# Moving a block's first transform steps within a fused Fourier-mixing and SoLU kernel, and reordering the float64 conversion in its opening

## The chip, the cores and the metric

The kernel runs on one core of a Trainium2 chip. The metric is the device time of one execution in microseconds; a lower number is better. Seven runs of the kernel before took 1685.17 to 1698.09 us, with a median of 1690.2 us.

## What is computed

The reference has two parts. The first filters each of 8 sequences of 3136 tokens by 256 channels in the frequency domain. The second is a feed-forward layer on all 25088 tokens: a product with `w_in` (256 by 1024), softmax-weighting of each value by itself (SoLU), a layer norm with gain `g_ln`, and a product with `w_out` (1024 by 256).

```python
X = np.fft.rfft(x, axis=1)                  # x: 8 x 3136 x 256
y = np.fft.irfft(X * (filt_r + 1j * filt_i)[None], n=3136, axis=1)
h = y.reshape(25088, 256) @ w_in            # w_in, w_out arrive as float64
e = np.exp(h - h.max(-1, keepdims=True))
solu = h * e / (e.sum(-1, keepdims=True) + 1e-9)
ln = (solu - mean) / np.sqrt(var + 1e-6) * g_ln
out = ln @ w_out
```

## The kernel before

**Two kinds of work.** Each of the 8 sequences (an "entry", `e` = 0 to 7) goes through a Fourier transform that is written as small matrix products. A *first step* (a DFT of 49 points) works on one of 8 pieces of the sequence; its result is stored to a DRAM scratch tensor `d1`. Seven *spectrum units* read `d1`, transform (`forward`), multiply by the filter (`multiply`), transform back (`inverse`) and store to `d2`. Eight *steps back* (`fetch_back`, `back`) read `d2` and fill the token buffer `y`. The feed-forward layer then works on the tokens of `y`, 128 at a time.

**The opening** (L360 to L562) does the whole transform of entry 0, for there is nothing to overlap it with. Beside it, the two weight matrices, which lie in DRAM as float64, are converted to float32 in eight pieces `j` = 0 to 7, four for `w_in` and four for `w_out`. `begin(j)` issues the load of the raw 32-bit words from GpSimd's DMA queue into one of 3 buffers (`raw`). `load_float64` then builds the float32 from the words: eight VectorE instructions (L381 to L393) for sign, exponent and the upper bits of the fraction, and, in `finish`, one ScalarE instruction (L396) and two GpSimd instructions (L397, L398) for the lower bits. The conversions of pieces 2 to 7 stand between the steps back of entry 0, whose 16 products (`py`, L353) are each evacuated by ScalarE (L356). Ahead of the steps back stand seven "idle products" (`idle_row(7, "idler")`, L534), which compute nothing that is used.

**The steps.** After the opening, a loop of 205 steps (L988) runs the feed-forward layer, one block of 128 tokens per step, software-pipelined: in step `k`, TensorE makes the products with `w_in` for block `k` (L682; every two blocks share seven products of half blocks, for which GpSimd makes sums first, `pair_sums`, L660), ScalarE and VectorE apply the exponential and the normalisation to block `k-2`, VectorE transposes block `k-3` (L740), and DMAs regroup it (L752). The products with `w_out` (L794) begin only at step 9 (`LAG`). The order of everything within a step is written out by hand in `step(k)`, so each engine's instructions stand in that order.

**Where the transform of entries 1 to 7 stands.** `PLAN` gives, for each entry, the steps at which its eight first steps, seven spectrum units and eight steps back are put. Entry 2 (the third entry) has its first steps at steps 1, 3, ... 15. For entries 2 to 7 a first step at step `t` is made of these parts:

- four loads of rows of `x` from SyncE's DMA queue (`fetch_quarters`, L236), into one of four buffers (`r`) that steps back also use. The load is put about three steps ahead; a load due before step 0 is issued ahead of the loop;
- a subtraction on VectorE (`difference`, L245), at the beginning of step `t`, into the only buffer of its kind (`diff`);
- an addition on GpSimd (`sum`, L251), in the middle of step `t`;
- eight products on TensorE (`first_quarters`, L260), four with `x` and four with `diff`, and two copies on ScalarE (L265), at the end of step `t`;
- two stores to `d1` from GpSimd's DMA queue (L271), at the beginning of step `t+1`.

Entry 1 is different: its first steps (L217) stand in steps 0 and 1, its rows were loaded by SyncE in the opening (`fetch_second`, L415; the last two pieces by GpSimd, L206), and its results are stored by GpSimd's queue (L223). Between `fetch_second` and the first rows of entry 2, SyncE's queue stores the filter to DRAM (`f_dram`, L543).

**The output weights** are also prepared in the first four steps: in step 0 they are scaled by `g_ln` (L618), in step 1 their mean over rows is made by 32 products (`ps_mean`, L626), in step 2 it is subtracted (L631), in step 3 the sums of quarters are made (L141).

Of the kernel before, what the change touches and what calls it, by code (L numbers as in the profile page):

```python
# [9 lines left out]
FP32 = mybir.dt.float32  # L10
I32 = mybir.dt.int32
AFT = mybir.ActivationFunctionType
ALU = mybir.AluOpType
# [23 lines left out]
PLAN = [  # L37
    None,
    ([0, 0, 0, 0, 1, 1, 1, 1], [4, 5, 6, 7, 8, 10, 12], [16, 17, 18, 19, 20, 20, 21, 22]),
    (range(1, 17, 2), range(18, 32, 2), [34, 36, 38, 40, 42, 43, 44, 46]),  # L40
    ([17, 23, 25, 27, 29, 31, 33, 35], range(38, 52, 2), range(54, 70, 2)),
    (range(39, 55, 2), range(58, 72, 2), range(76, 92, 2)),
    (range(63, 79, 2), range(82, 96, 2), range(100, 116, 2)),
    (range(87, 103, 2), range(106, 120, 2), range(126, 142, 2)),
# [48 lines left out]
def kernel(  # L93
# [10 lines left out]
    nc = tc.nc  # L104
# [6 lines left out]
    def pool(name, bufs, space=None, stack=ctx):  # L111
        kw = {} if space is None else {"space": space}
        return stack.enter_context(tc.tile_pool(name=name, bufs=bufs, **kw))
# [15 lines left out]
    w_in_sb = consts.tile([P, 7, DFF // 2], FP32, name="w_in_sb")  # L129
# [8 lines left out]
    def weight_sums(w):  # L138

        for to, a, b in ((3, 6, 0), (5, 2, 6), (4, 2, 3), (6, 1, 4)):  # L140
            nc.vector.tensor_tensor(out=w[:, to], in0=w[:, a], in1=w[:, b], op=ALU.subtract)  # L141
# [218 lines left out]
    with ExitStack() as st:  # L360
        fpool = pool("fp", 1, stack=st)
        pools = {name: pool(name + "0", bufs, stack=st)
                 for name, bufs in (("r", 1), ("t2", 1), ("p", 2), ("g", 2))}
        wpool = pool("wp", 3, stack=st)
        ps_h = pool("ps_h", 3, PSUM, stack=st)

        def load_words(src, n):
# [3 lines left out]
                in_=src)  # L371
            return raw

        def load_float64(dst, raw, negate=False):


            lo, hi = raw[:, :, 0], raw[:, :, 1]
            power = wpool.tile([P, 512], I32, name="power", tag="power", bufs=2)
            frac = dst.bitcast(I32)
            ts, stt = nc.vector.tensor_scalar, nc.vector.scalar_tensor_tensor  # L380
            ts(out=lo, in0=lo, scalar1=8, scalar2=None, op0=ALU.logical_shift_right)  # L381
            rest = lo.bitcast(FP32)
            ts(out=power, in0=hi, scalar1=20, scalar2=0x7FF, op0=ALU.logical_shift_right,
               op1=ALU.bitwise_and)
            ts(out=power, in0=power, scalar1=896.0, scalar2=0.0, op0=ALU.subtract, op1=ALU.max)
            ts(out=power, in0=power, scalar1=255.0, scalar2=None, op0=ALU.min)
            ts(out=power, in0=power, scalar1=23, scalar2=-2 ** 31 if negate else 0,
               op0=ALU.logical_shift_left, op1=ALU.bitwise_or)
            stt(out=power, in0=hi, scalar=-2 ** 31, in1=power, op0=ALU.bitwise_and,
                op1=ALU.bitwise_xor)  # L390
            ts(out=frac, in0=hi, scalar1=0xFFFFF, scalar2=3, op0=ALU.bitwise_and,
               op1=ALU.logical_shift_left)
            nc.vector.tensor_tensor(out=frac, in0=frac, in1=power, op=ALU.bitwise_or)  # L393

            def finish():
                nc.scalar.mul(rest, lo, 2.0 ** -44)  # L396
                nc.gpsimd.tensor_tensor(out=rest, in0=rest, in1=power.bitcast(FP32), op=ALU.mult)  # L397
                nc.gpsimd.tensor_tensor(out=dst, in0=dst, in1=rest, op=ALU.add)  # L398

            return finish  # L400

        filters, tables = {}, {}

# [23 lines left out]
        weights = []  # L427
# [18 lines left out]
        raws = {}  # L446

        def begin(j):
            raws[j] = load_words(weights[j][1], j)
# [40 lines left out]
        def idle_row(count, name):  # L490
            for j in range(count):
                idle(ps_h.tile([P, 2, C], FP32, name=f"{name}_{j}", tag="h"))
# [1 line left out]
        idle_row(8, "idle")  # L494

        def convert(j):
            return load_float64(weights[j][0], raws.pop(j), negate=j < 4)

        for j in range(2):
            convert(j)()  # L500

        def start(i):
            sp.fetch_filter(i)
# [15 lines left out]
        for i in range(units):  # L519
            if i + 2 < units:  # L520
                start(i + 2)
            sp.multiply(i, 0, nc.vector.tensor_tensor)
            sp.multiply(i, 1, nc.gpsimd.tensor_tensor)
            pss = [ps_t.tile([P, 2, C], FP32, name=f"pc_0_{i}_{u}", tag="t") for u in range(2)]
            idle(pss[0])
            sp.inverse(i, pss)
            sp.store(i, nc.scalar.dma_start)
            if i == 0:
                nc.gpsimd.dma_start(out=wi_t, in_=wi_dram)
                nc.gpsimd.dma_start(out=wq_t, in_=wq_dram)  # L530
                nc.gpsimd.dma_start(out=g_sb, in_=moe_g_ln.rearrange("(k p) -> p k", p=P))
            elif i in (1, 3, 4):
                begin({1: 2, 3: 3, 4: 4}[i])
        idle_row(7, "idler")  # L534
        rows_t4 = pools["r"].tile([P, NH, C], FP32, name="t4_0", tag="r")
        for ch in range(pieces):
            t4s[0, ch] = rows_t4[0:NK, NCH * ch:NCH * ch + NCH]
# [3 lines left out]
        for i0, n, rows in ((0, 4, P), (4, 4, P), (8, NP - 9, P), (NP - 1, 1, NQ)):  # L541
# [1 line left out]
            nc.sync.dma_start(  # L543
                out=f_dram[i0:i0 + n].rearrange("i u q k c -> (u q) i (k c)")[0:rows],
                in_=f[0:rows, at:at + n].rearrange("p i k c -> p i (k c)"))

        rest = {2: convert(2)}
        rest.pop(2)()
        begin(5)
        rest[3] = convert(3)  # L550
        for ch in range(pieces):
            if ch in (0, 2, 4, 6):
                j = 3 + ch // 2
                rest.pop(j)()
                if j < 5:
                    begin(j + 3)
                rest[j + 1] = convert(j + 1)
                if j == 3:
                    weight_sums(w_in_sb)
            for cb in range(KD):  # L560
                back(0, ch, cb, nc.scalar.copy)
        rest.pop(7)()  # L562


    ps_b = [pool(f"ps_b{u}", 1, PSUM) for u in range(2)]
# [270 lines left out]
    for e in range(1, B):  # L836
# [5 lines left out]
        for i, t in enumerate(first_at):  # L842
            dma = nc.gpsimd.dma_start
            if e == 1:
                if i not in sp.xs:
                    row_loads.append((t, t - 1, -1, lambda sp=sp, i=i, dma=dma: sp.fetch_x(i, [dma] * 2)))
                for u in range(2):
                    (early, late)[u][t].append(lambda sp=sp, i=i, u=u: sp.first(
                        i, (u,), psum(f"pa_{sp.e}_{i}_{u}").rearrange("p a c -> p (a c)").rearrange(
                            "p (o n) -> p o n", o=1), nc.scalar.copy, sp.xs[i][0:NK, 2 * u:2 * u + 2, :]))  # L850
                    (early, late)[u][t].append(lambda sp=sp, i=i, u=u: sp.store_first(
                        i, 2 * u, nc.gpsimd.dma_start))
            else:

                assert t % 2
                row_loads.append((t, t - 2, -1, lambda sp=sp, i=i: sp.fetch_quarters(i, nc.sync.dma_start)))
                stores[t].append(lambda sp=sp, i=i: sp.difference(i))
                products[t].append(lambda sp=sp, i=i: sp.sum(i))
                late[t].append(lambda sp=sp, i=i: sp.first_quarters(
                    i, [psum(f"pa_{sp.e}_{i}_{g}") for g in range(2)]))  # L860
                stores[t + 1].append(lambda sp=sp, i=i, dma=dma: sp.store_quarters(i, dma))
# [158 lines left out]
```

## Time and profile before

| | us |
|---|---|
| median of seven runs | 1690.2 |
| lowest and highest of them | 1685.17, 1698.09 |
| the profiled execution, its device time | 1696.86 |
| its span in the profile | 1695.1 |
| TensorE busy | 1603.3 (95%) |
| VectorE busy | 1264.7 (75%) |
| GpSimd busy | 1125.6 (66%) |
| ScalarE busy | 939.6 (55%) |
| mean granted TensorE clock | 0.982 |

In stages of the same execution, again in microseconds:

| stretch | TensorE busy | VectorE busy | GpSimd busy | granted clock |
|---|---|---|---|---|
| 0 to 100 | 68.00 | 50.38 | 46.28 | 0.91 |
| 100 to 200 | 80.12 | 64.14 | 57.62 | 0.82 |
| 200 to 300 | 94.42 | 76.93 | 75.30 | 0.99 |
| 300 to 400 | 96.50 | 78.06 | 65.53 | 1.00 |
| 1300 to 1400 | 99.42 | 76.05 | 69.00 | 1.00 |

In the tables and lines of the profile, PE is TensorE (PEld its weight loads), DVE is VectorE, ACT is ScalarE, POOL is GpSimd and SP is SyncE; SPq is SyncE's sequencer, which issues DMAs. A line of the timeline gives the start in microseconds from the beginning of the span, the duration, the engine, the line of the kernel, the operation, what it writes and reads, and in brackets how long the engine had been idle before it and what it waited for. Where two instructions are merged into one line, "x2" gives their number. A float32 product is two instructions on TensorE. The opening ends, and step 0 begins, at 110.9 us (the first `m` product, L682); step 2 begins at 148.8, step 10 at 219.5.

### The profile page before, as it was taken

What the parts mean: (1) busy time and instruction counts of PE and PEld (TensorE: products, weight loads), DVE (VectorE), ACT (ScalarE), POOL (GpSimd) and SP (SyncE); (2) the same over time, 40 slices, a digit from 0 to 9 for tenths busy, and PEclk for the clock granted to TensorE, in tenths of its full rate; (3) what the DMA queues carried; (4) which work ended last, traced back from release to release, by engine and by line L of the source; (5) the groups of instructions that cost most, each with busy time, mean ns of one, the idle gap of its engine ahead of it and who ended that gap; (6) DMA issues with size and microseconds to landing.
All of it is one profiled execution on the core that took longest, in us unless ns stands there. A gap on an engine that the chain in (4) does not pass through costs nothing.

```text
span 1695.1 us, 31047 instructions
## 1 busy us (share of the span) xinstructions
PE 1603.3 (95%) x10008; PEld 1099.3 (65%) x10008; DVE 1264.7 (75%) x2619; ACT 939.6 (55%) x1734; POOL 1125.6 (66%) x1272
## 2 busy tenths in 40 slices
PE   5787899999999999999999999999999999999996
PEld 1362356756766676667766676666776777777776
DVE  1684786788777878787778878787778777777772
ACT  2153546655656565556565665556565666656551
POOL 4463877568766765687567865688566766676664
PEclk8987999999999999999999999999999999999999
DMA  9885867877787767866787658766776444443443
GB/s 261 240 281 159 245 181 199 225 224 191 189 234 225 190 164 225 231 189 166 192 237 210 180 150 227 216 186 169 200 212 170 115 125 123 103 110 101 110 109 94
DMA packets 375957, 311.72 MB, mean 184 GB/s; under 512 B 61514, under 2 KB 341571, under 8 KB 375795
## 3 DMA queue, kind: packets, MB, share of 16 engines
q1 hardware_dynamic: 306260, 169.81, 38.3%
q0 software_dynamic: 32640, 101.65, 20.1%
q10 hardware_dynamic: 36896, 38.28, 8.0%
q8 instruction: 81, 1.33, 0.3%
q14 instruction: 80, 0.66, 0.1%
HBM read 124.83 MB, written 81.50 MB: 122 GB/s over the span
## 4 chain that ended last, share of the span: by engine, by line
PE 65%; DMA 15%; DVE 10%; SPq 3%; issue 3%; POOL 2%; ACT 1%; ACTq 0%; DVEq 0%; POOLq 0%
PE m L682 27%; PE o L794 26%; DMA solu_t<-turn 7%; PE py L353 5%; PE pa L260 3%; SPq L752 2%; PE pb L292 2%; DMA x<-in_x_dram 2%; PE pc L292 2%; DVE h L730 1%; DVE turn L740 1%; DMA t<-d 1%; DMA de<-de_tbl 1%; DVE diff L245 1%; PE pa L217 1%
## 5 line engine op out<-in xcount | busy, mean ns | idle before, releaser
L732 ACT ACTIVATE e<-h,nmu 128x1024 f32<-128x1024 f32 x196 | 225.4, 1150 | 365.3 <-DVE h L730 363.7
L794 PEld LDWEIGHTS o<-w_out_sb,solu_t 128*128 128x128 f32 x3136 | 381.2, 192 | 57.8 <-issue 39.7
L794 PE MATMUL o<-w_out_sb,solu_t 128*128 128x128 f32 x3136 | 401.7, 276 | 8.7 <-DVE rsum L725 5.5
L682 PE MATMUL m<-w_in_sb,s 128*128 128x512 f32 x784 | 401.1, 603 | 3.4 <-ACT h L692 3.1
L794 PEld LDWEIGHTS o<-w_out_sb,u 128*128 128x128 f32 x2352 | 305.3, 192 | 147.4 <-issue 112.1
L660 POOL TENSOR_TENSOR u<-solu_t 128x512 f32<-128x512 f32 x98 | 143.6, 1465 | 310.9 <-DMA solu_t<-turn 177.7
L682 PE MATMUL m<-w_in_sb,y 128*128 128x512 f32 x588 | 315.8, 621 | 22.3 <-DVE nmax L706 18.7
L794 PE MATMUL o<-w_out_sb,u 128*128 128x128 f32 x2352 | 313.3, 276 | 7.1 <-ACT ot L806 5.6
L730 DVE SCALAR_TENSOR_TENSOR h<-e,rsum,h 128x1024 f32<-128x1024 f32 x196 | 288.2, 1470 | 6.9
L813 DVE SCALAR_TENSOR_TENSOR ot<-o,rs_t,ot 128x128 f32<-128x128 f32 x294 | 102.5, 349 | 210.1 <-ACT ot L806 171.3
L692 ACT COPY h<-m 128x512 f32<-128x512 f32 x294 | 173.5, 590 | 128.6 <-PE m L682 113.4
L740 DVE STREAM_TRANSPOSE turn<-h 128x1024 f32<-128x1024 f32 x196 | 242.2, 1236 | 0.8
L714 ACT ACTIVATE e<-h,nmax 128x1024 f32<-128x1024 f32 x196 | 226.3, 1154 | 0.0
L660 POOL TENSOR_TENSOR u<-solu_t,u 128x512 f32<-128x512 f32 x98 | 142.8, 1457 | 88.6 <-PE o L794 84.4
L706 DVE CUSTOM_DVE_ANT_0 h<-m,h 128x512 f32<-128x512 f32 x196 | 133.0, 678 | 77.1 <-ACT h L692 52.1
L682 PEld LDWEIGHTS m<-w_in_sb,y 128*128 128x128 f32 x588 | 95.8, 193 | 131.7 <-DVE nmax L706 74.9
L353 PEld LDWEIGHTS py<-wi_t,t 100*128 100x128 f32 x1024 | 136.9, 198 | 56.4 <-issue 40.4
L682 PEld LDWEIGHTS m<-w_in_sb,s 128*128 128x128 f32 x784 | 124.3, 191 | 64.4 <-issue 46.1
L356 ACT COPY y<-py 128x392 f32<-128x392 f32 x128 | 109.1, 854 | 102.4 <-PE py L353 100.8
L660 POOL TENSOR_TENSOR solu_t<-solu_t,solu_t 128x512 f32<-128x512 f32 x98 | 151.8, 1549 | 7.7
L353 PE MATMUL py<-wi_t,t 100*128 100x98 f32 x1024 | 136.1, 279 | 3.8 <-ACT y L356 3.3
L660 POOL TENSOR_TENSOR u<-u,solu_t 128x512 f32<-128x512 f32 x98 | 136.8, 1396 | 0.7
(106 smaller groups left out, 1983.2 us busy)
## 6 DMA issues: line engine op xcount, KB each, us to landing
solu_t<-turn SPq DMA_DIRECT2D x784, 128.0 KB
out_dram<-ot SPq DMA_DIRECT2D x196, 128.0 KB
t<-d POOLq DMA_DIRECT2D x56, 400.0 KB, 5.1
d<-x POOLq DMA_DIRECT2D x100, 200.0 KB, 4.9
f<-f_dram POOLq DMA_DIRECT2D x39, 512.0 KB, 7.3
d<-g POOLq DMA_DIRECT2D x39, 512.0 KB, 4.7
t<-d ACTq DMA_DIRECT2D x36, 512.0 KB
x<-in_x_dram SPq DMA_DIRECT2D x112, 98.0 KB
```

The lines of the kernel that those rows point to most:

```text
L353: nc.tensor.matmul(out=psv[:, i:2 * NCH - i:2 * NCH - 1 - 2 * i, :], lhsT=t4s[e, ch][:, i, cb * P:cb * P + P], rhs=wi_t, start=True, stop= ...
L356: evac(out=y[:, cb, t0:t0 + S].rearrange("p (r m j) -> p m j r", m=N2 // NCH, j=NCH)[:, ch:last + 1 - ch:last - 2 * ch], in_=psv.rearrange ...
L660: nc.gpsimd.tensor_tensor(out=out, in0=in0, in1=in1, op=op)
L682: nc.tensor.matmul(out=ms[j, bank], lhsT=lhsT, rhs=w_in_sb[:, w, :], start=m in (1, 2, 7), stop=True, skip_group_check=True)
L692: nc.scalar.copy(out=h_half(k, i), in_=ms[j, 0])
L706: nc.vector.tensor_tensor_reduce(out=h_half(k, i), in0=ms[j, bank], in1=h_half(*kept), scale=1.0, scalar=sofar, op0=ALU.add, op1=ALU.min, ...
L714: nc.scalar.activation(out=e, in_=hs[k], func=AFT.Exp, bias=nmaxs.pop(k)[:, 1:2], scale=-1.0, accum_out=esum)
L730: nc.vector.scalar_tensor_tensor(out=solu, in0=e, scalar=rsum, in1=solu, op0=ALU.mult, op1=ALU.mult, accum_out=nmu)
L732: nc.scalar.activation(out=e, in_=solu, func=AFT.Square, bias=nmu, scale=-float(DFF), accum_out=variances[g][:, i:i + 1])
L740: nc.vector.transpose(out=turns[g][:, :, i, :], in_=solus.pop(k).rearrange("p (f j) -> p f j", j=32))
L794: nc.tensor.matmul(out=pos[p, bank], lhsT=lhs[:, f, :], rhs=w[:, f, :], start=f == 0 and m in (1, 2, 7), stop=True, skip_group_check=True)
L813: nc.vector.scalar_tensor_tensor(out=ot, in0=pos[p, bank], scalar=rs, in1=out_half(p, *kept)[0], op0=ALU.mult, op1=ALU.add)
```

## The change

It has three parts.

1. `PLAN`: the first steps of entry 2 move from steps 1, 3, 5, 7, 9, 11, 13, 15 to 3, 5, 7, 9, 10, 11, 12, 13; its spectrum units go from 18 to 30 to 16 to 28, its steps back from 34 to 46 to 32 to 46. One first step of entry 3 moves from step 17 to 15. Two first steps now stand at even steps (10 and 12), and the assertion against that is taken out.
2. Conversion: pieces 4 to 7 (the output weights) no longer use ScalarE or the GpSimd multiplication; one VectorE instruction makes the lower bits, and GpSimd only adds. For these pieces two VectorE instructions of the exponent become one. The raw words have five buffers. All conversions stand ahead of the steps back, and the loads of pieces 5 and 6 are issued two and more places earlier.
3. Fourteen idle products instead of seven stand ahead of the steps back.

```diff
@@ PLAN
-    (range(1, 17, 2), range(18, 32, 2), [34, 36, 38, 40, 42, 43, 44, 46]),
-    ([17, 23, 25, 27, 29, 31, 33, 35], range(38, 52, 2), range(54, 70, 2)),
+    ([3, 5, 7, 9, 10, 11, 12, 13], range(16, 30, 2), range(32, 48, 2)),
+    ([15, 23, 25, 27, 29, 31, 33, 35], range(38, 52, 2), range(54, 70, 2)),
@@ opening
-        wpool = pool("wp", 3, stack=st)
+        wpool = pool("wp", 5, stack=st)
@@ load_float64(dst, raw, negate, share)
-            ts(out=power, in0=power, scalar1=255.0, scalar2=None, op0=ALU.min)
-            ts(out=power, in0=power, scalar1=23, scalar2=-2 ** 31 if negate else 0,
-               op0=ALU.logical_shift_left, op1=ALU.bitwise_or)
+            if negate:
+                ts(out=power, in0=power, scalar1=255.0, scalar2=None, op0=ALU.min)
+                ts(out=power, in0=power, scalar1=23, scalar2=-2 ** 31, op0=ALU.logical_shift_left,
+                   op1=ALU.bitwise_or)
+            else:
+                ts(out=power, in0=power, scalar1=255.0, scalar2=2.0 ** 23, op0=ALU.min, op1=ALU.mult)
...
-            def finish():
+            if share:
                 nc.scalar.mul(rest, lo, 2.0 ** -44)
                 nc.gpsimd.tensor_tensor(out=rest, in0=rest, in1=power.bitcast(FP32), op=ALU.mult)
-                nc.gpsimd.tensor_tensor(out=dst, in0=dst, in1=rest, op=ALU.add)
-
-            return finish
+            else:
+                stt(out=rest, in0=lo, scalar=2.0 ** -44, in1=power.bitcast(FP32), op0=ALU.mult,
+                    op1=ALU.mult)
+            nc.gpsimd.tensor_tensor(out=dst, in0=dst, in1=rest, op=ALU.add)
@@ convert
-            return load_float64(weights[j][0], raws.pop(j), negate=j < 4)
+            load_float64(weights[j][0], raws.pop(j), negate=j < 4, share=j < 4)
@@ spectrum units of entry 0
-            elif i in (1, 3, 4):
-                begin({1: 2, 3: 3, 4: 4}[i])
-        idle_row(7, "idler")
+            elif i != 2:
+                begin({1: 2, 3: 3, 4: 4, 5: 5, 6: 6}[i])
+        idle_row(14, "idler")
@@ conversions and steps back of entry 0
-        rest = {2: convert(2)}
-        rest.pop(2)()
-        begin(5)
-        rest[3] = convert(3)
+        convert(2)
+        begin(7)
+        convert(3)
+        convert(4)
+        weight_sums(w_in_sb)
+        for j in (5, 6, 7):
+            convert(j)
         for ch in range(pieces):
-            if ch in (0, 2, 4, 6):
-                j = 3 + ch // 2
-                rest.pop(j)()
-                if j < 5:
-                    begin(j + 3)
-                rest[j + 1] = convert(j + 1)
-                if j == 3:
-                    weight_sums(w_in_sb)
             for cb in range(KD):
                 back(0, ch, cb, nc.scalar.copy)
-        rest.pop(7)()
@@ the steps
-                assert t % 2
```

The order in which the changed kernel's instructions stand differs in two more places. On SyncE's queue only the rows of one first step of entry 2, not of two, follow the filter's store, and they are put at the end of step 0 instead of ahead of it. On GpSimd the four load issues for the last rows of entry 1 (L206) come before the four sums for step 0 (L660), not after them.

## The prediction, made before the changed kernel ran

> **What bounds the kernel now.** I began with the slices of the page.
>
> ```profile
> PE   5787899999999999999999999999999999999996
> POOL 4463877568766765687567865688566766676664
> PEclk8987999999999999999999999999999999999999
> ```
>
> A slice is 42.4 us. From the sixth on TensorE is busy at nine tenths or more, at full clock: from there it is the bound, and work moved among full steps wins or loses only what it does to stalls. The first five slices, to about 210 us, are where time can be had. The windows and the timeline say where in them.
>
> ```profile
> 97.20:100.50 3.30, 0.04 (x1) 0.00 (x0) 3.16 (x8) 1.39 (x3) 0.69 (x1) 0.80 1.02 282
> 100.50:111.00 10.50, 10.46 (x49) 10.46 (x50) 10.26 (x14) 5.39 (x7) 5.38 (x4) 0.50 0.50 171
> ...
> 128.00:138.00 10.00, 3.61 (x7) 1.27 (x6) 2.06 (x5) 0.61 (x2) 4.85 (x9) 0.77 0.40 146
> ```
>
> Columns: stretch, length, then PE, PEld, DVE, ACT and POOL busy, granted clock, DMA share, GB/s. There are two holes: in 97.2 to 100.5 TensorE stands still, and after it the clock is 0.50 for 10.5 us; in 128 to 138 it works 3.61 us of 10. The first is the opening's:
>
> ```profile
> 98.61 0.42 DVE L381 TENSOR_SCALAR raw<-raw 128x512 int32<-128x512 int32 x1
> 99.11 0.67 ACT L396 ACTIVATE raw<-raw 128x512 f32<-128x512 int32 x1 [3.33 <-DVE raw L381]
> 100.54 10.31 PEld L353 LDWEIGHTS py<-wi_t,t 100*128 100x128 f32 x48 [3.46 <-ACT y L356]
> ```
>
> ScalarE's instruction for weight piece 5 waits for VectorE, behind it wait the copies of the steps back, and for those TensorE. The second hole:
>
> ```profile
> 134.68 0.69 DVE L245 TENSOR_TENSOR diff<-x 113x512 f32<-113x512 f32 x1 [14.30 <-DMA x<-in_x_dram]
> 136.03 2.07 PE L682 MATMUL m<-w_in_sb,y 128*128 128x512 f32 x2 [6.39 <-DVE nmax L706]
> 150.87 0.69 DVE L706 CUSTOM_DVE_ANT_0 h<-m,h 128x512 f32<-128x512 f32 x1 [11.96 <-PE m L682]
> ```
>
> Entry 2's first difference stands at the head of step 1 on VectorE; its rows land only at 134.6. All of VectorE's step 1 waits 14.3 us behind it, TensorE 6.4 of them. The rows are late because they follow the filter's store on SyncE's queue:
>
> ```profile
> 117.73 12.67 SPq L236 DMA_DIRECT2D x<-in_x_dram  x8
> SPq L236 <- DMA f_dram<-f: 8.1, 4, 4.8
> ```
>
> **The opening, worked out.** Seven more idle products: seven are 14 instructions from 80.39 to 86.6, 6.0 us at 0.43 each. Steps back then start at 92.6, not 86.6. They lose ScalarE's waits: ten of the sixteen took 86.6 to 97.2, 1.06 each, so sixteen take 17.0 and end at 109.6 against 111.1. The cover for the idle products is the landing of the pieces: in before the fifth of eight lands at 95.25 and they are issued 0.8 to 2.4 us apart, so the eighth lands near 102. Loads of weight pieces 5 to 7 come 9 to 11 us earlier; before, they were in this stretch too (85.8, 90.8, 97.1), so the bytes ahead of the eighth hardly grow. I allow 4 us (two loads, 1 MB at the stretch's 250 GB/s), to 106; it is wanted at 92.6 + 14.8 = 107.4. Gain for TensorE 1.5 us, from 0 (pieces 2 us later) to 2.
>
> VectorE: a conversion undisturbed takes 3.94 us (the first, 20.32 to 24.26); with two GpSimd additions or multiplications beside it 4.8 to 6.8 (82.3, 89.0, 98.7, 103.5, 109.4, 115.1 begin or end one). Pieces 2 and 3 stay. For each of 4 to 7, one instruction of 0.46 goes, one that no row shows comes: scalar, tensor, 128x512. The nearest, L389, takes 0.61 to the next start; bounds 0.35 (L391) and 1.47 (twice as wide, L730): I take 0.61, since it has the same operands. Piece 4: 6.0 + 0.15; sums 3.6; pieces 5 to 7 with one GpSimd addition instead of two instructions beside them: 4.1, 5.1, 5.1. From 89.0: 113.1 against 115.05. With 1.47 four times it is 116.5, a loss of 1.5. The Trainium skill, "SBUF — State Buffer" (on the port that VectorE and GpSimd share), speaks against the new instruction: two inputs in SBUF make it wait for a GpSimd instruction that holds the port. The rows show such a delay, L393 taking 0.69 or 1.67; by the rule all four could pay 0.98, and VectorE would end at 117.0.
>
> GpSimd's queue takes back what this gives. Its last addition ends at 114.5 instead of 117.70. But the four load issues (2.8 us, 117.99 to 120.79) now precede step 0's sums, of which the product that began at 118.51 needs two (1.0 us): 114.5 + 0.3 + 2.8 + 1.0 = 118.6. So I count the opening as 0 at that product; bounds -2 (sums hold nothing) and +3 (GpSimd no earlier than before).
>
> **Steps 0 and 1.** From that product to step 2's first (118.51 to 148.84) the trace has 30.3 us. Out go: the 6.4 us of waiting; eight products of entry 2 (142.61 to 144.5, 1.9); the slow clock after the hole, in which two `m` and four `pa` take 2.07 and 3.00 instead of 1.02 and 1.88 (2.2); and 0.4 of the 0.73 wait for their copies. Sum 10.9. Next late is what the same stretch holds otherwise: rows of entry 1's last pieces (used at 126.3 and 127.7, requested at 118.0, now 3 us earlier) and GpSimd's sixteen stores, which no longer wait 4.9 us behind L251. The first difference now stands at step 3, 156.4 - 10.9 = 145.5; its rows, asked for at the same place of SyncE's queue and with nothing of a second unit behind them, should land by 134.6: 11 us to spare. If they came after 145.5, VectorE would wait again. Steps 2 to 9 keep their work (a unit at every odd step from 3), so they should merely begin 10.9 us sooner.
>
> The Trainium skill, "TensorE: Matmul & The Clock Gate" (Part 1), lets the clock fall to half after an idle window of about 3.4 us, windows running free. This trace agrees: 3.30 us of standstill, then 0.50. By that rule idle products buy clock only if the gaps left in steps 0 and 1 stay under it; a gap of some 2 us is left before the sums, and one window cold would cost 1.7, an estimate from that page.
>
> **Steps 9 to 16.** The unit that leaves step 1 comes back among full steps, at 10 and 12 against 15 (entry 3's unit, 17 to 15, moves between full steps and costs nothing of itself). On the path it costs TensorE 1.9 us. Beside the path it brings SyncE four issues (2.1), GpSimd an addition and two issues (1.27 + 1.07), VectorE 0.94, ScalarE 1.07. Units now stand in five steps running, 9 to 13. In 210 to 260 GpSimd is busy 38.7 of 50 us and VectorE 43.4; two additional units take 4.7 and 1.9 of what is free. What late GpSimd costs, the trace shows:
>
> ```profile
> 266.16 0.65 PE L260 MATMUL pa<-x,wq_t 49*64 49x512 f32 x2 [1.12 <-POOL x L251]
>   POOL x L251: 8.4, 8
> ```
>
> The second row is from L260's own view to 520 us: of 19 units eight waited, 8.4 us together, 1.05 a wait. SyncE's regroup loads wait behind the new row loads; GpSimd's sums (L660) wait for those. I put 1.5 us on stalls, between 0 and 5 (all five waiting at 1.05). The buffer of differences, one only, is free when TensorE has done the unit of the step before, 218.5 to 219.5; VectorE comes to step 10's at 219.7, so nothing is priced there. Entry 2's spectrum units two steps earlier overlap four of entry 3's units, not five: 0, from -2 to +2.
>
> **Sum.** 0 - 10.9 + 1.9 + 1.5 = -7.5 us. The profiled execution took 1696.86 (span 1695.1 and 1.8 around it), so it would take 1689.4. It lies 6.7 above the median; against that the same difference gives 1690.2 - 7.5 = 1682.7.
>
> **Rivals.**
> *GpSimd's queue holds step 0.* The wait is gone, but another takes its place: if the last addition ends as late as before, 117.7, the sums come 3.1 us later, TensorE stands more than 3.3 us, and 10.5 us follow at half clock, 5.2 lost: 10.9 - 8.3 = 2.6, less 3.4 for the units, +0.8, or 1691.0. For it: loads ahead of sums in that queue. Against it: GpSimd loses four multiplications of 1.35. It decides from an addition ending after 116.6.
> *Five units in a row.* Slower: if each of the units of steps 9 to 13 waits for GpSimd's whole 2.34 (11.7) and one gap halves the clock (5.2), 16.9 + 1.9 - 10.9 = +7.9, 1698.1. It decides once stalls there pass 9.0. For it: GpSimd at 77% and VectorE at 87% in these steps. Against it: free time is twice the need, and waits have been 1.05.
>
> **Chances.** Forecast 0.66, the queue 0.21, five units 0.13. Forecast alone spans -10.9 (no stalls, 1.9 of the opening kept) to -3, so 1679 to 1687; a few us of scatter are in any median. With the first rival whole and a part of the second, 8 in 10 lie in 1675 to 1693. 0.3% is 5.1 us, about what a measurement of this kernel tells from no change. Faster: most of the forecast and a little of the queue, 0.63; same 0.23; slower 0.14.
>
> **What would show it.** Right: no VectorE wait for rows of `x` before step 3; `py` products without a standstill, at clock 1.0, from about 92.6; step 2's first `m` near 138; step 10 near 209; L260's waits for L251 in steps 9 to 13 under 5 us together. Wrong: step 2 later than 144, a standstill above 3.3 us before `m` of step 0 is through, half clock anywhere after 112, or step 16 no longer 7 us ahead.

## The result, and the profile after

The changed kernel takes 1684.8 us (median of 17 runs, 1678.91 to 1692.42) against 1693.3 for the kernel before, measured beside it (44 runs, the seven from before the change among them). The ratio is 0.9949, with a 95% interval of 0.9935 to 0.9963: the medians lie 8.5 us apart, where 7.5 had been forecast. A second comparison gave 0.9955 [0.9935, 0.9975]. The profiled execution took 1690.85 us, its span 1689.0; against the profiled execution before that is 6.0 us.

The slices of the page come first, as before:

```profile
PE   5798899999999999999999999999999999999996
POOL 4444777577666756787577866677566666667664
PEclk8998899999999999999999999999999999999998
```

A slice is 42.2 us. TensorE's third and fourth slices (84 to 169 us) went from 8 and 7 to 9 and 8. GpSimd's third went from 6 to 4: its multiplications are gone. The clock's fourth slice went from 7 to 8, but its fifth fell from 9 to 8: that was not forecast, and comes back below.

The windows over the two places where the holes had been (columns as before: stretch, length, then PE, PEld, DVE, ACT and POOL busy, granted clock, DMA share, GB/s):

```profile
91.50:108.10 16.60, 16.19 (x130) 14.85 (x128) 16.19 (x27) 12.93 (x16) 4.50 (x3) 1.00 0.74 214
124.00:136.00 12.00, 12.00 (x48) 6.03 (x47) 2.22 (x6) 5.39 (x10) 6.71 (x14) 1.00 0.68 228
```

The steps back run through at clock 1.00, and in the last 12 us ahead of step 2 TensorE is busy all the time. The timeline of the opening's end:

```profile
79.40 12.28 PE L492 MATMUL idler<-f,de 128*128 128x512 f32 x28
91.52 16.51 PE L353 MATMUL py<-wi_t,t 100*128 100x98 f32 x128
108.09 2.06 PE L680 MATMUL m<-w_in_sb,y 128*128 128x512 f32 x4
110.18 0.69 DVE L403 SCALAR_TENSOR_TENSOR raw<-raw,power 128x512 f32<-128x512 int32 x1
110.94 1.29 POOL L405 TENSOR_TENSOR w_out_sb<-w_out_sb,raw 128x512 f32<-128x512 f32 x1 [3.68 <-DVE raw L403]
112.52 2.67 POOL L206 DMA_DIRECT2D x<-in_x_dram  x4 [0.29 <-DMA y<-in_x_dram]
116.33 3.21 PE L680 MATMUL m<-w_in_sb,s 128*128 128x512 f32 x4 [1.93 <-POOL s L658]
```

Read it downwards: the idle products end where the steps back begin, and these end 3 us earlier than before. VectorE's last conversion instruction (L403, the new one) starts at 110.18 and GpSimd's last addition ends at 112.2. Then GpSimd's queue issues four loads (L206) before it makes the sums (L658), and TensorE's first product with a sum waits for those: 1.93 us of idleness in the bracket, at 116.33 against 118.51 before.

SyncE's queue and VectorE's first difference for entry 2:

```profile
107.15 7.97 SPq L548 DMA_DIRECT2D f_dram<-f  x4
115.43 4.75 SPq L236 DMA_DIRECT2D x<-in_x_dram  x4
144.17 0.68 DVE L245 TENSOR_TENSOR diff<-x 113x512 f32<-113x512 f32 x1
```

The difference now stands at step 3 and its line has no bracket: VectorE didn't wait. Only four row loads follow the store, not eight. Step 2's first `m` starts at 136.57 (148.84 before).

To see where a lead is won and lost I compared the start of the squaring in each step's normalisation (ScalarE, L730; L732 in the kernel before) in both profiles, and took the changed kernel's time minus the time before:

| step | 2 | 5 | 8 | 10 | 12 | 14 | 17 | 18 | 31 | 46 | 92 | 192 |
|---|---|---|---|---|---|---|---|---|---|---|---|---|
| us | -12.3 | -12.3 | -10.0 | -10.0 | -6.3 | -5.3 | -2.1 | -3.5 | -8.3 | -7.1 | -8.8 | -7.9 |

So 12.3 us are won ahead of step 2, 2.3 are lost in steps 5 to 7, 7.9 in steps 10 to 16, and 5.0 of those come back by step 46, from when on both kernels have done the same work. After that the two executions drift by up to 1.7 us. Two windows show what the loss in steps 10 to 16 is. The kernel before:

```profile
225.60:281.30 55.70, 53.25 (x323) 36.25 (x322) 44.13 (x93) 31.36 (x60) 43.29 (x49) 1.00 0.70 189
```

and the changed kernel, over the same steps:

```profile
215.60:279.20 63.60, 57.88 (x360) 37.60 (x359) 52.29 (x99) 33.10 (x64) 48.02 (x56) 1.00 0.74 202
```

TensorE is busy 4.6 us longer with 37 more instructions: the unit that left step 1, and one of entry 3 and a part of a spectrum unit, which the kernel before does after step 16. It is idle 5.7 us instead of 2.4: 3.3 us more of stalls. The waits of TensorE in those steps of the changed kernel:

```profile
PE o L792 <- DVE rsum L723: 2.9, 2, 1.7
PE pa L260 <- POOL x L251: 1.6, 1, 1.6
```

Columns: who waited for whom, us in all, times, the longest. GpSimd's sums cost 1.6 (1.1 before). The larger term is the wait for VectorE's row sums, 2.9 (0.4 before): VectorE is busy 82% of this stretch, 79% before.

### The profile page after: what moved, and what is told of

Same layout as the page of the kernel before. It is cut to its first block, busy times and chain, and to the rows that moved or that the text cites. A ratio compares the mean times of both kernels' runs of the same rounds, so it can differ in the third digit from the quotient of the medians.

```text
span 1689.0 us, 31072 instructions
## 1 busy us (share of the span) xinstructions
PE 1603.4 (95%) x10022; PEld 1098.2 (65%) x10022; DVE 1270.5 (75%) x2619; ACT 937.7 (56%) x1730; POOL 1117.2 (66%) x1268
## 4 chain that ended last, share of the span: by engine, by line
PE 68%; DMA 16%; DVE 6%; POOL 3%; issue 3%; SPq 2%; ACT 2%; ACTq 0%; DVEq 0%; POOLq 0%
PE m L680 27%; PE o L792 27%; DMA solu_t<-turn 6%; PE py L353 5%; DMA x<-in_x_dram 2%; PE pb L292 2%; PE pa L260 2%; PE pc L292 2%; DMA t<-d 2%; SPq L750 2%; PE pa L217 1%; DVE h L728 1%; DMA de<-de_tbl 1%; POOL u L658 1%; DVE turn L738 1%
## 5 line engine op out<-in xcount | busy, mean ns | idle before, releaser
L730 ACT ACTIVATE e<-h,nmu 128x1024 f32<-128x1024 f32 x196 | 225.3, 1150 | 369.7 <-DVE h L728 367.9
L792 PEld LDWEIGHTS o<-w_out_sb,u 128*128 128x128 f32 x2352 | 306.3, 192 | 147.9 <-issue 110.9
L658 POOL TENSOR_TENSOR u<-solu_t 128x512 f32<-128x512 f32 x98 | 142.3, 1452 | 309.9 <-DMA solu_t<-turn 154.8
L680 PE MATMUL m<-w_in_sb,y 128*128 128x512 f32 x588 | 315.8, 621 | 16.1 <-DVE nmax L704 12.7
L728 DVE SCALAR_TENSOR_TENSOR h<-e,rsum,h 128x1024 f32<-128x1024 f32 x196 | 293.9, 1500 | 6.9
L690 ACT COPY h<-m 128x512 f32<-128x512 f32 x294 | 173.5, 590 | 130.0 <-PE m L680 117.7
L658 POOL TENSOR_TENSOR u<-solu_t,u 128x512 f32<-128x512 f32 x98 | 142.2, 1451 | 90.9 <-PE o L792 86.8
L353 PEld LDWEIGHTS py<-wi_t,t 100*128 100x128 f32 x1024 | 132.3, 192 | 53.9 <-issue 39.9
L658 POOL TENSOR_TENSOR solu_t<-solu_t,solu_t 128x512 f32<-128x512 f32 x98 | 150.1, 1532 | 7.7
L658 POOL TENSOR_TENSOR u<-u,solu_t 128x512 f32<-128x512 f32 x98 | 138.9, 1417 | 0.7
L353 PE MATMUL py<-wi_t,t 100*128 100x98 f32 x1024 | 131.6, 273 | 0.7 <-DMA t<-d 0.4
```

The source lines that it names most:

```text
L353: nc.tensor.matmul(out=psv[:, i:2 * NCH - i:2 * NCH - 1 - 2 * i, :], lhsT=t4s[e, ch][:, i, cb * P:cb * P + P], rhs=wi_t, start=True, stop= ...
L658: nc.gpsimd.tensor_tensor(out=out, in0=in0, in1=in1, op=op)
L680: nc.tensor.matmul(out=ms[j, bank], lhsT=lhsT, rhs=w_in_sb[:, w, :], start=m in (1, 2, 7), stop=True, skip_group_check=True)
L690: nc.scalar.copy(out=h_half(k, i), in_=ms[j, 0])
L728: nc.vector.scalar_tensor_tensor(out=solu, in0=e, scalar=rsum, in1=solu, op0=ALU.mult, op1=ALU.mult, accum_out=nmu)
L730: nc.scalar.activation(out=e, in_=solu, func=AFT.Square, bias=nmu, scale=-float(DFF), accum_out=variances[g][:, i:i + 1])
```

## The experiments

In the diffs, line numbers are left out. Each ratio is against the kernel before, measured beside it.

**The schedule alone.** The changed `PLAN` (and the dropped assertion) in the kernel before, with its old opening.

> The new PLAN with the old opening. Theory (the row wait at step 1 is the gain): no wait of VectorE for rows of x at step 1; step 2's first product with w_in near 138.5 (before 148.8, less the 10.1 us that the changed kernel won between step 0's first product with a sum and step 2); ratio to before about 0.9963, some 6 us. Rival (the opening's standstill and half clock carry the gain): ratio between 0.999 and 1.001, because 97 to 111 us stays as it was and the wait at step 1 hid behind other work.

Measured: 1682.2 us, ratio 0.9950 [0.9932, 0.9968], the same as the whole change. VectorE has no wait for rows. From the first product with a sum (122.30) to step 2's first `m` (141.08) it takes 18.8 us, against 30.3 before and 20.2 in the changed kernel. That `m` comes 2.6 us later than I expected, for in this execution the product with a sum came 3.8 us later than in the kernel before. So the schedule is the whole gain that a comparison can see, and a little more than I gave it.

**The opening alone.** The changed opening, with the old `PLAN`.

> The new opening with the old PLAN. Theory: the rows of entry 2 still follow the filter's store, which now begins 3 us earlier (107.2 against 110.2), so VectorE waits for them until about 131.5; step 2's first product near 146; ratio 0.998 to 0.999, 2 to 3 us. Rival (the opening carries the gain): step 2 near 141, ratio 0.996 or less.

Measured: 1691.8 us, ratio 1.0012 [0.9993, 1.0032]. It missed: there is no gain. The timeline shows why; rows, queue and VectorE's wait stand side by side:

```profile
107.91 2.08 PE L680 MATMUL m<-w_in_sb,y 128*128 128x512 f32 x4
116.12 17.34 SPq L236 DMA_DIRECT2D x<-in_x_dram  x8
135.35 0.69 DVE L245 TENSOR_TENSOR diff<-x 113x512 f32<-113x512 f32 x1 [19.07 <-DMA x<-in_x_dram]
```

Step 0 begins 3 us earlier (110.89 before), but the rows, requested 1.6 us earlier, land at 135.3 (134.6 before; I had expected 131.5). VectorE's wait has grown from 14.3 to 19.1 us, and TensorE's behind it from 6.4 to 9.8. An earlier start ahead of a transfer that lands no earlier buys nothing; why the rows gain nothing by the earlier request isn't shown.

**One unit alone.** The old opening, and only entry 2's first unit moved to step 10.

```diff
-    (range(1, 17, 2), range(18, 32, 2), [34, 36, 38, 40, 42, 43, 44, 46]),
+    ([3, 5, 7, 9, 10, 11, 13, 15], range(18, 32, 2), [34, 36, 38, 40, 42, 43, 44, 46]),
```

> The opening of the kernel before, and of the schedule only one move: entry 2's first unit goes from step 1 to step 10 (3, 5, 7, 9, 10, 11, 13, 15); spectrum units, steps back and entry 3 as before. Theory (all of the gain is the wait for rows at step 1, and the unit costs TensorE its products at step 10): VectorE waits for no rows in steps 0 to 2, step 2 begins 8 to 11 us after the kernel before's lead is counted, ratio 0.9945 to 0.9965, the same as the whole schedule's 0.995. Rival (five units in a row and the earlier spectrum units cost some us that this kernel doesn't pay): 0.991 to 0.993, and the lead still at 6 us or more at step 17, where the kernel with the whole schedule had none.

Measured: 1683.0 us, ratio 0.9942 [0.9923, 0.9961], just below the theory's range; its interval holds the whole schedule's 0.995 and reaches into the rival's range. In its profile VectorE waits for no rows, step 2 leads by 10.6 us, and at step 17 the lead is still 14.1, as the rival had it. The window over steps 10 to 16:

```profile
211.20:267.20 56.00, 54.63 (x333) 36.49 (x332) 45.81 (x93) 32.43 (x62) 44.57 (x52) 1.00 0.75 202
```

56.0 us against 55.7 before, though TensorE does one unit more: it is busy 1.4 us longer, and idle 1.4 instead of 2.4. In this execution the unit filled gaps. The times of this kernel and of the whole schedule can't be told apart, so the remainder of the schedule (step 12, entry 3's unit, the earlier spectrum) is worth nothing that these comparisons show. Most of what it costs by step 17, it pays back: from step 10 to step 46 the lead falls by 1.4 us here and by 2.4 with the whole schedule.

**Sums first.** The changed kernel with GpSimd's four sums of step 0 ahead of its four loads.

```diff
+    first_loads = []
...
-            load()
+            first_loads.append(load)
...
         pair_sums(0)
+        for load in first_loads:
+            load()
```

> The changed kernel, with GpSimd's four sums for step 0 put ahead of its four load issues for entry 1's last rows. Theory (that queue holds back 2 us of the opening's gain): the 1.93 us wait of step 0's product for the sum goes, everything after comes 1.9 us sooner, ratio to before near 0.9938. Rival: the rows of entry 1's last pieces, asked for 2 us later, become late for step 1 (used at 125.9), and the ratio stays near 0.995.

Measured: 1678.7 us, ratio 0.9931 [0.9915, 0.9948]. The timeline has the sums directly behind the additions, and no bracket at the product:

```profile
112.73 0.45 POOL L658 TENSOR_TENSOR s<-y 128x128 f32<-128x128 f32 x1
114.99 1.88 PE L680 MATMUL m<-w_in_sb,s 128*128 128x512 f32 x4
```

From the first `m` (109.24) to this product it takes 5.75 us, where the changed kernel takes 8.24. I repeated the pair on one chip:

> The changed kernel once more, beside the next one on the same chip: ratio 0.9935 to 0.9965, as it was.

> The changed kernel with GpSimd's sums of step 0 ahead of its four loads once more, on the chip of the last one. Theory (the loads held step 0 by 1.9 us and by the clock that the gap cost): 2 to 4 us below the changed kernel, ratio 0.9915 to 0.9945. Rival (its lower median was scatter): within 1 us of the changed kernel.

Measured: 1688.1 and 1684.9 us, ratios 0.9955 [0.9935, 0.9975] and 0.9931 [0.9904, 0.9958]. The repeat is 3.2 us lower, and the profiles of both pairs show the product earlier, by 2.5 and 1.9 us (5.75 and 6.59 from the first `m`, against 8.24 and 8.47). The intervals overlap: likely, and not settled.

**The store from another queue.** The opening alone, with the filter's store issued by ScalarE after its last copy of the opening.

```diff
-            nc.sync.dma_start(
+            nc.scalar.dma_start(
```

> The new opening with the old PLAN, and the filter's store moved from SyncE's queue, where it stood ahead of entry 2's first rows, to the end of the opening on ScalarE's queue. Theory (the store ahead of them made the rows late): rows asked for at about 112.5, landed by about 122, VectorE waits 2 us at most at step 1, step 2's first product near 138.5; as the first unit stays where TensorE has time, ratio about 0.994. Rival (the DMA engines are full at 110 to 125 us whatever the queue): the rows land at 130 or later and the ratio is that of the new opening alone, 0.998 to 0.999.

Measured: 1692.7 us, ratio 1.0007 [0.9990, 1.0025]. The theory missed: the rows landed at 133.6. But the run doesn't answer the question, for SyncE was then held earlier (SyncE's waits):

```profile
SPq L420 <- DMA f_dram<-f: 8.9, 2, 8.0
```

By the profile the loads of entry 1's rows waited for a store that is on another queue now. What was taken from one place of SyncE's queue came back in another.

**A quarter of the store.** The kernel before, in which each of the filter's stores writes a quarter of its bytes; loads and stores keep their number and their place.

```diff
-    f_dram = dram.tile([NP, 2, NQ, 2, C], FP32, name="f_dram")
+    f_dram = dram.tile([P, NP, P], FP32, name="f_dram")
...
-                out=f_dram[i0:i0 + n].rearrange("i u q k c -> (u q) i (k c)")[0:rows],
-                in_=f[0:rows, at:at + n].rearrange("p i k c -> p i (k c)"))
+                out=f_dram[0:rows, i0:i0 + n],
+                in_=f[0:rows, at:at + n, 0, 0:P])
...
-            in_=f_dram[i:i + pairs].rearrange("i u q k c -> (u q) i (k c)")[0:rows])
+            in_=f_dram[0:rows, i:i + 1].broadcast_to([rows, 4 * pairs, P]))
```

> The kernel before with a quarter of the filter's store: 0.8 MB instead of 3.2 between the rows of entry 1 and those of entry 2 on SyncE's queue; later entries read the quarter four times, so their filter is not the reference's. Theory (the rows of entry 2 are late because the store's bytes are ahead of them): the store's four issues stay, the rows of step 1's unit land by 127 instead of 134.6, VectorE's wait at its head falls from 14.3 to under 8 us, TensorE's 6.4 us behind it to under 1, ratio 0.994 to 0.997. Rival (something else holds them: the lanes that the row loads share with entry 1's rows, or the other loads and stores of the stretch): rows land at 132 or later, wait of 11 us or more, ratio 0.998 to 1.001.

Measured: 1687.4 us, ratio 0.9952 [0.9929, 0.9975]. The timeline:

```profile
109.62 6.59 SPq L543 DMA_DIRECT2D f_dram<-f  x4
117.34 4.96 SPq L236 DMA_DIRECT2D x<-in_x_dram  x8
126.23 0.69 DVE L245 TENSOR_TENSOR diff<-x 113x512 f32<-113x512 f32 x1 [5.89 <-DMA x<-in_x_dram]
```

The first rows are requested as late as before (117.3 and 117.7) but land at 126.2 instead of 134.6, VectorE's wait is 5.9 us instead of 14.3, and TensorE has none behind it. All eight issues take 5.0 us instead of 12.7, for SyncE no longer waits for the store between them (8.1 us before). So the store's bytes made the rows late; whether on the way or by SyncE's waits for the store, this run doesn't separate. Without touching the schedule this alone gives about what the change gives. In 110 to 120 us the kernel before keeps the DMA engines at a share of 0.96 with 364 GB/s, this one at 0.67 with 223.

**Seven idle products.** The changed kernel with half of its idle products.

```diff
-        idle_row(14, "idler")
+        idle_row(7, "idler")
```

> The changed kernel with seven idle products in place of fourteen ahead of the steps back. Theory (the idle products cover the wait for the first rows of the steps back and keep the clock, but step 0 is set by GpSimd's and VectorE's chain, not by TensorE): the idle products end near 85.5, TensorE stands 3 to 6 us, steps back run at half clock for up to 10 us and step 0's first m comes 0 to 4 us later than 108.1, while the product with a sum stays within 1.5 us of 116.3; ratio 0.995 to 0.9965. Rival (the idle products are what the opening gains by): the product with a sum comes 3 us or more later and the ratio is 0.997 or above. Rival 2 (they do nothing): clock 0.9 or more throughout, the same times.

Measured: 1691.5 us, ratio 0.9979 [0.9966, 0.9993]. The first rival was right, not my theory. The windows of the standstill and of the steps back:

```profile
85.90:90.70 4.80, 0.00 (x0) 0.00 (x0) 4.70 (x6) 0.00 (x0) 2.67 (x2) 0.77 0.91 281
90.70:118.20 27.50, 27.46 (x129) 27.49 (x130) 20.25 (x34) 12.68 (x15) 8.43 (x8) 0.50 0.84 271
```

TensorE stands 4.8 us for the first rows, and then all 128 instructions of the steps back run at clock 0.50: 27.5 us where the changed kernel takes 16.5. Step 0's first `m` comes at 118.13 (108.09), the product with a sum at 125.60 (116.33). I had expected a half clock "for up to 10 us".

But the kernel before has seven idle products too, and its steps back began at 86.62 without a wait. What is late is SyncE's request for the first rows: 1.8 to 2.3 us after the idle products begin in the four kernels with the old opening, 5.6 to 6.9 us in the nine with the new one (85.03 against 79.40 in the changed kernel, 82.27 against 80.39 before). SyncE waits there for the store of the last spectrum unit, and the new opening issues two loads of weights ahead of that store, at 75.4 and 77.3. The next experiment puts them back.

**Late loads.** Seven idle products, and the loads of weight pieces 5 and 6 behind the conversion of piece 2.

```diff
-            elif i != 2:
-                begin({1: 2, 3: 3, 4: 4, 5: 5, 6: 6}[i])
-        idle_row(14, "idler")
+            elif i in (1, 3, 4):
+                begin({1: 2, 3: 3, 4: 4}[i])
+        idle_row(7, "idler")
...
         convert(2)
+        begin(5)
+        begin(6)
         begin(7)
```

> The changed kernel with seven idle products, and the loads of weight pieces 5 and 6 issued behind the conversion of piece 2, next to that of piece 7, instead of among the spectrum units. Theory (the earlier loads stand ahead of the last spectrum unit's store, so that SyncE asks for the first rows of the steps back 5.6 to 6.9 us after the idle products begin, where the kernels with the old loads ask after 1.8 to 2.3; the seven additional idle products only cover this): rows asked for 2 to 3 us after, the steps back begin within 1 us of the idle products' end at clock 0.9 or more, m of step 0 at 105 to 109, ratio 0.994 to 0.997, where the same kernel with the early loads had 0.9979 and a half clock of 27.5 us. Rival (the rows are late by something else in the new opening): asked for 5 us or more after, a standstill of 4 us and the half clock again, 0.997 to 0.999.

Measured: 1684.7 us, ratio 0.9931 [0.9905, 0.9957], below the theory's range, into which its interval reaches; the seven idle products that weren't enough in the kernel above are enough here. TensorE's timeline:

```profile
77.99 6.28 PE L492 MATMUL idler<-f,de 128*128 128x512 f32 x14
84.27 2.00 PE L353 MATMUL py<-wi_t,t 100*128 100x98 f32 x16
...
100.38 7.12 PE L353 MATMUL py<-wi_t,t 100*128 100x98 f32 x32 [0.53 <-DMA y<-in_x_dram]
```

The rows are asked for at 79.66, 1.7 us after the idle products begin, and the steps back start without a wait. Only the clock didn't keep to the forecast: later steps back wait for DMAs four times, 0.4 to 1.3 us each, and in 100 to 110 us the granted clock is 0.50. Still the steps back end at 107.5. So the earlier weight loads made the first rows late, and the seven additional idle products of the change cover a wait that the change itself brings.

**The unit at step 2, and the unit at step 4.** Sums first, and entry 2's first steps at 2, 3, 5, ..., 15, or at 3, 4, 5, 7, ..., 15, the rest of `PLAN` as before. The diff is that of the first; the second differs from it only in these numbers.

```diff
-    ([3, 5, 7, 9, 10, 11, 12, 13], range(16, 30, 2), range(32, 48, 2)),
-    ([15, 23, 25, 27, 29, 31, 33, 35], range(38, 52, 2), range(54, 70, 2)),
+    ([2, 3, 5, 7, 9, 11, 13, 15], range(18, 32, 2), [34, 36, 38, 40, 42, 43, 44, 46]),
+    ([17, 23, 25, 27, 29, 31, 33, 35], range(38, 52, 2), range(54, 70, 2)),
```

> The changed kernel with GpSimd's sums of step 0 ahead of its four loads, and entry 2's first steps at 2, 3, 5, 7, 9, 11, 13, 15, all else of the schedule as before the change: the unit of step 1 moves by one step alone, no unit is added to full steps. Theory (rows land by 133 to 135 whatever the queue, and step 2's difference comes at about 133): VectorE waits 0 to 3 us for rows at step 2, no unit of 1.9 us is paid at steps 10 to 13, ratio 0.990 to 0.993 against 0.9931 for the same kernel with the changed schedule. Rival (the wait simply moves on with the unit, 6 us or more at step 2): 0.994 to 0.998.

> As the last one, but entry 2's first steps at 3, 4, 5, 7, 9, 11, 13, 15: the unit of step 1 goes to step 4, where there is no product with the output weights yet. Theory (in steps 3 to 9 TensorE runs at 0.83 to 0.93 of its clock and has gaps, so a unit there costs less than its 1.9 us; in full steps it costs all): no wait for rows, the lead at step 17 is 10 us or more, ratio 0.990 to 0.9925. Rival (TensorE pays the unit wherever it stands, and the earlier spectrum units of the changed schedule were worth something later): 0.993 to 0.995, no better than the changed schedule.

Measured: 1681.1 us, 0.9925 [0.9908, 0.9942], and 1683.6 us, 0.9928 [0.9915, 0.9942]. Both intervals hold "sums first" (0.9931). With the unit at step 2 the wait moves on with it, as the rival had it; the rows land at 141.0, not at 133 to 135 (timeline):

```profile
140.97 0.69 DVE L245 TENSOR_TENSOR diff<-x 113x512 f32<-113x512 f32 x1 [13.80 <-DMA x<-in_x_dram]
143.06 1.19 PE L260 MATMUL pa<-x,wq_t 49*64 49x512 f32 x2 [5.95 <-POOL x L251]
```

VectorE waits 13.8 us, TensorE 6 behind it, and step 2 leads by 9.2 us instead of the 15.0 of "sums first". Still the time is no worse; why, these runs don't show. With the unit at step 4 there is no wait, and the window over steps 10 to 16 has the length that it had before the change:

```profile
212.30:268.00 55.70, 53.14 (x323) 36.16 (x322) 45.78 (x93) 31.25 (x60) 44.46 (x49) 1.00 0.69 189
```

The lead is 13.2 us at step 6 and 13.3 at step 17, as its theory said; yet the ratio lies between the two ranges, and within 0.0003 of "sums first". At step 46, where all have done the same work, the profiled executions lead by 6.5 us (unit at step 2), 14.6 (unit at step 4) and 11.7 ("sums first"; 13.1 in the repeat), and the three ratios lie within 0.0006 of one another. By these comparisons they are equal. Each beats the kernel before, and each lies 0.002 below the changed kernel with intervals that just overlap; which is the best is open.

## Why the prediction was right, point by point

*The wait for rows* (6.4 us of TensorE, and with it 10.9 for steps 0 and 1). Right in mechanism and size: 19.4 was forecast, and 30.3 us became 20.2 in the changed kernel (18.6 in its second execution), 18.8 with the old opening, 18.9 with sums first. The reason given, the filter's store ahead of the rows, was right as far as the store's bytes go: storing a quarter of them brought the rows forward by 8.4 us. That it is the place on SyncE's queue isn't shown; the run that changed the queue was confounded.

*The opening: 0 at the product with a sum.* It came at 116.33 (116.96 in the second execution) instead of 118.6, 2.2 earlier than before and just beyond the lower bound of -2. Two terms were too cautious by 1 to 2.3 us: the steps back began at 91.5 (92.6 forecast) and ended at 108.0 (109.6); the conversions ended at 110.9 (113.1) and the last addition at 112.2 (114.5). The chain behind them was as forecast: 112.2 + 0.3 + 2.7 + 1.1 = 116.3. That those loads held step 0 is shown by "sums first". In time no gain of the opening shows: with the old schedule the rows' landing eats it (1.0012), and with the new one the ratios are 0.9950 without it and 0.9949 with it, with intervals wide enough to hide 2 us.

*The gap before the sums.* "Some 2 us" it was: 1.93 in both executions of the changed kernel. In the profiled one the clock fell behind it, and the next instructions came at half clock:

```profile
119.34 4.16 PE L217 MATMUL pa<-y,wf_t 98*100 98x512 f32 x8
```

The product ahead of this line took 3.21 us. In the second execution the same two took 1.99 and 3.66, at a clock of 1.00. So a gap below the 3.3 us of the prediction's sign brought the half clock in one execution and not in the other. It cost 1.7 us, what the prediction had put on it, and makes the difference between 20.2 and 18.6 above.

*The price of the new VectorE instruction.* I took 0.61 us from one start to the next; it is 0.60, with a busy time of 0.69 for all four. None of the four was delayed, for GpSimd was idle when they started; so the rule on two inputs that the prediction weighed (the Trainium skill, "SBUF — State Buffer", on the shared port) had no case here. The delay of about a microsecond was there, but it fell on an instruction with one input, two places further on, when GpSimd's addition had begun: L383 took 1.52 us beside it and 0.42 alone.

*The idle products, and the loads that come earlier.* "The bytes ahead of the eighth hardly grow" was the wrong question: it is the first piece that the earlier loads delay, by some 4 us, since its request waits for a store behind them. I counted 1.5 us of gain for TensorE and no such delay; the loads came 10 to 13.5 us earlier, not 9 to 11. That it came out right is luck: the seven additional idle products end where the first piece lands (91.5). With the loads early and no such cover, the steps back take 27.5 us and the ratio goes from 0.995 to 0.998.

*Steps 2 to 9 "merely begin 10.9 us sooner".* Wrong by 2.3 us in the profiled execution, where the same instructions ran at different clocks. The kernel before, over steps 4 and 5, and 6 and 7:

```profile
169.00:187.70 18.70, 16.17 (x90) 6.74 (x89) 14.69 (x30) 9.19 (x17) 13.81 (x16) 0.91 0.73 233
187.70:207.40 19.70, 15.81 (x87) 6.29 (x87) 14.57 (x28) 9.47 (x17) 17.04 (x18) 0.91 0.86 254
```

and the changed kernel:

```profile
156.40:176.70 20.30, 17.76 (x90) 7.00 (x88) 14.88 (x30) 9.15 (x16) 13.82 (x16) 0.83 0.75 224
176.70:197.40 20.70, 16.96 (x87) 7.09 (x87) 14.63 (x28) 9.53 (x17) 17.06 (x18) 0.84 0.81 251
```

As many products, 2.6 us more. Both kernels stand for GpSimd's `pi` in these steps, 5.5 us in two waits of up to 3.0. Windows of 1 us show a clock of 0.50 for 3.4 us at or just behind each of the two in the kernel before, and for 6.8 us at each in the changed kernel. The second execution of the changed kernel had 3.4 and 6.8, and lost 1.1 us in steps 5 to 7 instead of 2.3. In the stretches 160 to 180 and 180 to 200 us the kernel with the old opening and the new schedule had 0.91 and 0.83, "sums first" 1.00 twice: the clock around such waits changed from one execution to the next, and here the changed kernel had the lower one. The prediction's step treated it as given. Its sign of being wrong, "half clock anywhere after 112", came true, but the kernel before had a half clock in these steps too, so the sign couldn't tell the two apart.

*Steps 9 to 16: 1.9 for the unit and 1.5 for stalls.* The stalls were 3.3, within 0 to 5, but mostly not where I had put them: GpSimd's sums cost 0.5 more, VectorE's row sums 2.5 more. From step 10 to step 46, where the work is equal again, the lead falls by 2.9 us; 3.4 had been forecast. What I had not said is that the lead falls to 2.1 us on the way, because the schedule does a unit and some spectrum earlier. "Step 16 still 7 us ahead" failed for that reason (3.2), without telling anything of the end.

*The rivals.* GpSimd's queue did hold step 0, but the last addition ended at 112.2, far from the 116.6 from which that was to decide. Five units in a row waited 1.6 us for GpSimd, where 9.0 would have been needed.

*The sum.* By the profiled execution: -12.3 ahead of step 2, +2.3 in steps 5 to 7, +2.9 to step 46, together -7.1, of which 6.1 are left at the end; between the medians it is -8.5, for a forecast of -7.5. The opening's 2.2, which had been counted as 0, and the colder clock's 2.3 cancelled, and that is luck: in the second execution the same sum is -13.3 ahead of step 2, +0.5 to step 10 and +3.4 to step 46, together -9.4. The -3 at the upper end of the forecast's span is not the sum of its bounds: stalls of 5 us alone give -4.0, and with the opening's +3 it is -1.0.

## What to carry to other kernels

Before you make a start earlier, look for the transfer whose landing the next stage waits for: here 3 us won in the opening were worth nothing while the next stage waited for a transfer that landed no earlier, and cutting a store ahead of that transfer to a quarter of its bytes gained as much as the whole change. A lead read a few steps behind a moved unit mixes time with work done ahead; compare where both kernels have done the same work. When a load is issued earlier, look which store it now stands ahead of, and who waits for that store.

## What was not expected of the hardware

*A half clock that busy products don't lift.* With seven idle products TensorE was busy 27.46 of 27.5 us at a granted clock of 0.50. The Trainium skill, "TensorE: Matmul & The Clock Gate" (Part 1), has the full clock come back after some 3.4 us of sustained work; these rows disagree. In that stretch the weight loads too were busy all the time (27.49), the products being only 98 columns wide; the same products kept the full clock in the changed kernel, where they began at it.

*A half clock comes and goes between executions of the same steps.* Around GpSimd's `pi`, with waits of up to 3.0 us in both, the clock over two steps was 0.91 in one profile and 0.83 in the other, worth 2.6 us. The lengths are not arbitrary: summed from windows of 1 us, every stretch at 0.50 between 80 and 220 us, in the profiles of both kernels and of all twelve experiments, lasts 3.4 us or a whole multiple of it (6.8, 10.2, 13.7, 17.1, and 34.1 with seven idle products). At these two waits it was one such length or two, and which of them differed between executions.
